# Two constants of a list scheduler: a longer hand-over between engines is counted, and attention's TensorE work is ranked further ahead

## The chip, the cores and the metric

The kernel runs on one core of one Trainium2 chip. The metric is device time in microseconds (us), from one execution to the next, as a median over runs. Engines are called by the profile's names: PE is TensorE (matmuls; PEld its weight loads), DVE is VectorE, ACT is ScalarE, POOL is GpSimd, SP is SyncE, which here only issues the transfers (DMA).

## What is computed

Three stages feed one another: local attention with block summaries (2 batches, 8 heads, 768 positions, head width 64), and two MLPs (1536 tokens, 512 wide, 2048 inside), the first with softplus and the second with a squared ReLU. All is float32.

```
k_sum = k.reshape(B, H, nb, 32, D).max(axis=3)
v_sum = v.reshape(B, H, nb, 32, D).mean(axis=3)
scores_l = scale * q @ k^T, kept where |i - j| < 16
scores_s = scale * q @ k_sum^T + log(32)
a = softmax over [scores_l, scores_s];  attn = a @ [v, v_sum]
x = attn as (1536 tokens, 512)
x = softplus(x @ w_in) @ w_out          (moe)
x = relu(x @ w_in)**2 @ w_out           (moe2)
```

## The kernel before

**The work.** Attention goes over 12 tiles of 128 tokens, t0 to t11 (t0 to t5 are batch 0), each with 24 summary keys and two windows of 96 keys. The queries and keys come in blocks u0 to u5 of 256 tokens. For a block, `tr` transposes on PE (line L361; the first blocks at L397) and copies the result out of PSUM (ACT or DVE, L306 or L308); for keys `kmax` (L369) also takes block maxima on DVE. For a tile, `tile_sc` multiplies queries with keys (L491), and the softmax follows: the mask is added on DVE (L499), the maximum taken on DVE (L530), subtracted on POOL (L532), exponentiated on ACT (L534), summed on DVE (`tot`, L516 to L518) and scaled on POOL (L536). `tile_px` transposes the weights of the softmax in two halves (L547, copied out at L306 or L308), multiplies them with the values (L561), and splits the product into a high part `xh` (L306) and a low part `xl` (L571). `vsum_mm` (L439, copied out at L444) makes the block means of the values once for each batch.

An MLP product takes three matmuls, high times high, high times low, low times high. Each weight block (a step c of 128 inner columns, in and out weight) is therefore split first: ACT or DVE extracts the lowest three bits (L609 on ACT, L611 on DVE), DVE joins bits twice (L614), ACT or POOL scales and copies (L306 or L308), and POOL or DVE subtracts for the low part (L623). `mlp_in` multiplies tokens with the in weight (L664), ACT applies the function (L671) and copies the high part (L678), DVE takes the low part (L680), and `mlp_out` multiplies with the out weight (L701). The first MLP's steps c0 to c3 run on 256 tokens at a time while attention is still going on (stretch A below); all other steps run on 512 tokens.

**What sets the order.** The program collects all operations in a `Plan`, each with the engines that can do it, a duration for each, a due time, and what it reads and writes. `Plan.run` goes through them once, when the program is built. It keeps a clock for each engine, always takes the engine that can start first, and from the operations that are ready on it the one with the earliest due time. Where two engines can do an operation, the one that would end first gets it. A result counts as ready for others at its end plus `SEM`. So the plan's numbers set only an order of instructions for each engine and the choice of engine. On the chip each engine works through its order and waits at each instruction for its inputs. `PEB` is taken off the due time of attention's PE operations alone:

```
op("PE", 0.65, due - PEB, mm, r=[("s", y, hh), "id"], w=[bk], take=bk)
...
ready[u] = max(ready[u], end + self.SEM)
```

`Plan.run` also fills holes: where the plan sees PE idle for over 0.9 us, it puts matmuls that compute nothing there (`warm`, L857). PSUM space for attention's results (the tiles `ab`; the first tiles also use `h`) is handed out in the plan's order; from t2 on there are two such tiles, and a new product has to wait until the old one has been copied out. Transfers are issued from SP in the plan's order; raw weight blocks (`raw`, four places) at L599 and L602, windows of values (`vwin`) at L425, blocks of queries and keys at L350.

## Time and profile before

| | |
|---|---|
| median of 3 runs | 619.96 us (619.87 to 622.35) |
| the profiled execution, its time | 620.8 us |
| its span, first to last instruction | 619.0 us |
| PE busy | 602.5 us (97%) |
| DVE busy | 312.1 us (50%) |
| ACT busy | 288.2 us (47%) |
| POOL busy | 202.0 us (33%) |

1.8 us of the profiled execution lie outside the span. Busy shares are means over the whole span; PE's includes the matmuls that compute nothing.

### The profile page before, as it was taken

How to read it: one execution, taken by the hardware profiler on the slowest of the kernel's cores; microseconds unless marked ns; L12 is line 12 of the kernel's file. 1: busy time of each engine (PE TensorE's matmuls, PEld its weight loads, DVE VectorE, ACT ScalarE, POOL GpSimd, SP SyncE). 2: the span in 40 equal slices, each digit the busy share in tenths (PEclk: the TensorE clock that was granted, in tenths of full speed). 3: DMA queues.
4: the chain of work that ended last, by engine and by line, in shares of the span. 5: the costliest groups of instructions: out<-in, count | busy, mean ns of one | idle time of the engine just before them, and what ended most of it. 6: DMA issues, size and time to landing. Idle time of an engine off the chain costs nothing.

```text
span 619.0 us, 9449 instructions
## 1 busy us (share of the span) xinstructions
PE 602.5 (97%) x3809; PEld 507.5 (82%) x3809; DVE 312.1 (50%) x449; ACT 288.2 (47%) x501; POOL 202.0 (33%) x197
## 2 busy tenths in 40 slices
PE   9798999999999999999999999999999999999996
PEld 7687988999788888888888888888888888888885
DVE  5788999726664133542146652247542533232332
ACT  4686888856653124542247643346412432221220
POOL 5877696535550042331138440116000410000000
PEclk9798999999999999999999999999999999999999
DMA  9999632423541014340024330114100100010011
GB/s 283 243 281 217 162 74 55 116 69 116 166 128 35 0 35 136 103 136 1 0 64 122 120 103 0 35 61 131 47 1 0 69 0 2 0 58 11 20 50 68
DMA packets 64524, 51.34 MB, mean 83 GB/s; under 512 B 36320, under 2 KB 58848, under 8 KB 64480
## 3 DMA queue, kind: packets, MB, share of 16 engines
q1 hardware_dynamic: 64480, 50.73, 28.6%
q8 instruction: 30, 0.49, 0.3%
q14 instruction: 14, 0.11, 0.1%
HBM read 47.58 MB, written 3.15 MB: 82 GB/s over the span
## 4 chain that ended last, share of the span: by engine, by line
PE 84%; DVE 8%; DMA 4%; ACT 2%; SPq 1%; issue 1%; POOL 0%; DVEq 0%; POOLq 0%
PE h L664 40%; PE accp L701 21%; PE acc L701 18%; DMA late<-in_v_dram 2%; DMA vwin<-in_v_dram 2%; DVE raw L614 2%; DVE mx L530 1%; DVE s L499 1%; PE ab L439 1%; PE ab L561 1%; DVE sm L516 1%; SPq L382 1%; PE ab L547 1%; DVE xl L571 0%; DVE sm L517 0%
## 5 line engine op out<-in xcount | busy, mean ns | idle before, releaser
L664 PE MATMUL h<-xh,wih 128*128 128x512 f32 (+1 forms) x432 | 159.9, 370 | 0.0
L664 PE MATMUL h<-xh,wil 128*128 128x512 f32 (+1 forms) x432 | 158.7, 367 | 0.0
L664 PE MATMUL h<-xl,wih 128*128 128x512 f32 (+1 forms) x432 | 158.7, 367 | 0.0
L614 DVE SCALAR_TENSOR_TENSOR raw<-raw 128x512 uint32<-128x512 uint32 x128 | 113.3, 902 | 52.8 <-ACT raw L609 39.8
L664 PEld LDWEIGHTS h<-xh,wih 128*128 128x128 f32 x432 | 81.5, 189 | 14.6 <-issue 0.6
L664 PEld LDWEIGHTS h<-xh,wil 128*128 128x128 f32 x432 | 81.3, 188 | 13.9
L664 PEld LDWEIGHTS h<-xl,wih 128*128 128x128 f32 x432 | 81.4, 188 | 13.7
L673 ACT ACTIVATE e<-h 128x512 f32<-128x512 f32 x48 | 28.8, 599 | 125.4 <-PE h L664 125.4
L675 DVE SCALAR_TENSOR_TENSOR h<-h,e 128x512 f32<-128x512 f32 x48 | 33.5, 698 | 103.2 <-ACT e L673 103.1
L671 ACT ACTIVATE h<-h 128x512 f32<-128x512 f32 (+1 forms) x60 | 29.8, 499 | 83.2 <-PE h L664 83.1
L308 POOL TENSOR_SCALAR wih<-raw 128x512 fp32r<-128x512 f32 x18 | 12.6, 703 | 150.5 <-PE h L664 142.1
L623 POOL TENSOR_TENSOR wol<-raw,woh 128x512 fp32r<-128x512 f32 x30 | 42.6, 1421 | 48.9 <-ACT woh L306 48.3
L623 POOL TENSOR_TENSOR wil<-raw,wih 128x512 fp32r<-128x512 f32 x31 | 42.6, 1374 | 28.9 <-ACT wih L306 27.4
L609 ACT ACTIVATE raw<-raw 128x512 uint32<-128x512 uint16 x59 | 39.3, 670 | 13.2 <-DMA raw<-in_moe_w_out_dram 7.5
L680 DVE TENSOR_TENSOR g1l<-h,g1h 128x512 fp32r<-128x512 f32 (+1 forms) x40 | 24.2, 606 | 31.9 <-ACT g1h L678 31.8
L723 DVE TENSOR_TENSOR part<-accp,part 128x512 f32<-128x512 f32 x24 | 16.0, 686 | 43.5 <-PE accp L701 43.5
L680 DVE TENSOR_TENSOR g2l<-h,g2h 128x512 fp32r<-128x512 f32 x28 | 19.3, 690 | 33.7 <-ACT g2h L678 33.5
L306 ACT ACTIVATE raw<-raw 128x512 f32<-128x512 f32 x41 | 27.5, 673 | 18.7 <-DVE raw L614 18.7
L680 DVE TENSOR_TENSOR g0l<-h,g0h 128x512 fp32r<-128x512 f32 (+1 forms) x40 | 24.1, 605 | 21.1 <-ACT g0h L678 20.9
L678 ACT ACTIVATE g0h<-h 128x512 fp32r<-128x512 f32 (+1 forms) x40 | 21.2, 534 | 16.4 <-DVE h L675 16.0
L536 POOL TENSOR_TENSOR s<-s,sm 128x960 f32<-128x960 f32 (+1 forms) x14 | 22.1, 1580 | 13.9 <-DVE sm L518 13.0
L678 ACT ACTIVATE g1h<-h 128x512 fp32r<-128x512 f32 (+1 forms) x40 | 21.4, 534 | 9.2 <-DVE h L675 8.9
(172 smaller groups left out, 1175.4 us busy)
## 6 DMA issues: line engine op xcount, KB each, us to landing
raw<-in_moe_w_in_dram SPq DMA_DIRECT2D x32, 512.0 KB, 4.2
raw<-in_moe_w_out_dram SPq DMA_DIRECT2D x32, 512.0 KB, 3.4
vwin<-in_v_dram SPq DMA_DIRECT2D x20, 192.0 KB, 5.7
part<-in_k_dram SPq DMA_DIRECT2D x12, 256.0 KB, 4.9
late<-in_v_dram SPq DMA_DIRECT2D x2, 1536.0 KB, 11.3
out_dram<-part SPq DMA_DIRECT2D x12, 256.0 KB, 2.1
part<-in_q_dram SPq DMA_DIRECT2D x10, 256.0 KB, 5.1
vwin<-in_v_dram SPq DMA_DIRECT2D x4, 160.0 KB, 5.2
```

What stands on the lines that cost most here:

```text
L306: nc.scalar.activation(out=out_, in_=in_, func=AF.Copy, **({} if mul is None else {"scale": mul}))
L536: op(("POOL", "DVE"), (1.8 * n + 0.1, 1.75 * n), due, lambda e, sv=sv, rv=rv, spread=spread: tt(e).tensor_tensor(out=sv, in0=sv, in1=sprea ...
L609: nc.scalar.activation(out=lo, in_=q4[:, :, 1], func=AF.Copy, scale=2.0 ** -13, bias=-4095.5 / 8192.0)
L614: nc.vector.scalar_tensor_tensor(out=lo, in0=hi, scalar=n, in1=lo, op0=how, op1=ALU.bitwise_or)
L623: op(("POOL", "DVE"), (1.4, 1.0), dv, lambda e: tt(e).tensor_tensor(out=ws[s][kl], in0=lo.bitcast(F32), in1=ws[s][kh].bitcast(F32), op=ALU ...
L664: nc.tensor.matmul(out=hview(st), lhsT=ws[s][wn][:, w_], rhs=xx[bl][:, kk, o:o + n], start=(kk == 0 and xx is xh and wn == "ih"), stop=(kk ...
L671: op("ACT", ta, due, lambda: nc.scalar.activation(out=hview(st), in_=hview(st), func=AF.Softplus), w=[H_], tab="sp")
L673: op("ACT", ta, due, lambda: nc.scalar.activation(out=e_t[st["g"] % 2], in_=hview(st), func=AF.Relu), r=[H_], w=[("e", st["g"] % 2)])
L675: op("DVE", tv, due, lambda: nc.vector.scalar_tensor_tensor(out=hview(st), in0=hview(st), scalar=0.0, in1=e_t[st["g"] % 2], op0=ALU.max, o ...
L678: op("ACT", ta, due, lambda: nc.scalar.activation(out=gview(st)[0], in_=hview(st), func=AF.Copy), r=[H_] + need, w=gk[0])
L680: op("DVE", tv, due, lambda: nc.vector.tensor_tensor(out=gview(st)[1], in0=hview(st), in1=gview(st)[0].bitcast(F32), op=ALU.subtract), r=[ ...
L701: nc.tensor.matmul(out=o, lhsT=a[:, sl], rhs=b, start=(st["first"] and c == 0 and not (A and m % 2)), stop=(st["last"] and c == 2 and not ...
```

## The change

Both edits are numbers. `SEM` is the time that the plan counts between the end of an operation and the start of one that needs it on any engine. `PEB` is the lead that attention's PE operations get in rank over all other PE operations.

```
-PEB = 40.0
+PEB = 60.0
...
-    SEM = 0.12
+    SEM = 0.3
```

The set of computing operations is the same; their order on each engine, the engine of some of them, and the number of filling matmuls change (53 before, 50 after). Over the whole program these choices differ: the bit extraction runs 59 times on ACT and 5 times on DVE before, 63 times and once after; the low part of a weight 61 times on POOL and 3 times on DVE before, 64 times and never after; one transposed block is copied by DVE before, and three PSUM results of `tile_px` after. The loads of ACT's function tables are 18 in both.

On ACT, where the softmax of t3 (tile `s_133`) meets the second weight block of c2 (`raw_76`, the out weight), this is the order before:

```order
L671 ACTIVATE h_109<-h_109 128x256
L306 ACTIVATE kT<-ab_141 128x4x128
L678 ACTIVATE g0h<-h_109 128x256
L306 ACTIVATE qT_127<-ab_142 128x4x128
L534 ACT_TABLE_LOAD
L534 ACTIVATE s_133<-s_133 128x960
L306 ACTIVATE at_134<-ab_141 120x512
```

And this is the order after, at the same place:

```order
L306 ACTIVATE kT<-ab_141 128x4x128
L671 ACTIVATE h_109<-h_109 128x256
L609 ACTIVATE raw_76<-raw_76 128x512
L306 ACTIVATE qT_127<-ab_142 128x4x128
L678 ACTIVATE g0h<-h_109 128x256
L534 ACT_TABLE_LOAD
L534 ACTIVATE s_133<-s_133 128x960
L306 ACTIVATE at_134<-ab_142 120x512
```

The bit extraction of `raw_76`, which DVE did before, stands on ACT ahead of the copy of a query block, of c1's high part and of t3's exponentials.

On DVE the piece of the difference at the same place shows what left and what stayed (`raw_75` to `raw_77` are the blocks of c2's in, c2's out and c3's in weight):

```order
-L680 TENSOR_TENSOR g0l<-h_109,g0h 128x256
-L614 SCALAR_TENSOR_TENSOR raw_75<-raw_75 128x512
-L611 TENSOR_SCALAR raw_76<-raw_76 128x512
+L680 TENSOR_TENSOR g0l<-h_108,g0h 128x256
+L614 SCALAR_TENSOR_TENSOR raw_75<-raw_75 128x512
+L614 SCALAR_TENSOR_TENSOR raw_76<-raw_76 128x512
+L680 TENSOR_TENSOR g0l<-h_109,g0h 128x256
 L611 TENSOR_SCALAR raw_77<-raw_77 128x512
+L499 TENSOR_TENSOR s_132<-sc,mask 128x480
 L516 TENSOR_REDUCE sm_139<-s_133 128x8
```

The extraction of `raw_77` stays on DVE ahead of t3's sum (L516); that of `raw_76` is gone, and c1's low part (`g0l<-h_109`) now stands behind a join of `raw_76`.

On PE the piece of the difference a little later, where t2's weighted values (L561) and the block means of batch 1 (L439) are made:

```order
 L701 MATMUL accp<-g0h,wol_90 128x256
 L701 MATMUL accp<-g0l,woh_89 128x256
-L361 MATMUL ab_141<-ident,part_69 128x128 x4
+L547 MATMUL ab_142<-ident,s_132 120x128 x4
+L439 MATMUL ab_141<-late,sel 24x128 x24
 L561 MATMUL ab_142<-at_134,vwin_130 64x64 x16
-L439 MATMUL ab_141<-late,sel 24x128 x24
 L664 MATMUL h_108<-xh_71,wih_91 128x256
```

The block means moved ahead of t2's weighted values, and the second half of t2's transposes came down to just ahead of them; the query block's transposes went further up, out of this piece.

## Rows read from the trace of the kernel before

**Rows 1.** The page, part 1: busy us, share of the span, instructions.

```profile
PE 602.5 (97%) x3809; PEld 507.5 (82%) x3809; DVE 312.1 (50%) x449; ACT 288.2 (47%) x501; POOL 202.0 (33%) x197
```

**Rows 2.** Windows: stretch and length, each engine's busy us, then PE's granted clock, DMA.

```profile
22.00:28.50 6.50, 6.50 (x70) 5.26 (x71) 5.09 (x12) 3.00 (x10) 4.81 (x6) 0.56 0.92 199
48.00:56.40 8.40, 6.04 (x95) 4.88 (x94) 7.32 (x10) 3.82 (x9) 4.28 (x5) 0.80 1.01 207
...
60.90:104.00 43.10, 40.56 (x540) 37.52 (x536) 42.76 (x61) 35.81 (x58) 33.38 (x29) 1.00 0.46 109
104.00:146.75 42.75, 42.38 (x464) 41.26 (x465) 24.88 (x41) 30.44 (x54) 18.70 (x15) 1.00 0.30 83
146.75:619.00 472.25, 466.97 (x2066) 384.00 (x2064) 198.82 (x278) 181.76 (x311) 107.18 (x92) 1.00 0.18 58
```

**Rows 3.** The waits of PE over the span: total us, times, longest us.

```profile
PE ab L439 <- DMA late<-in_v_dram: 3.3, 1, 3.3
...
PE accp L701 <- ACT part L713: 0.6, 1, 0.6
```

**Rows 4.** Timeline of PE, 22 to 29 us: start, us, instructions [idle before].

```profile
22.00 2.78 PE L439 MATMUL ab<-late,sel 128*24 128x128 f32 x48 [3.33 <-DMA late<-in_v_dram]
24.70 2.10 PE L857 MATMUL h<-ident 128*128 128x256 bf16 x9
...
28.05 0.60 PE L857 MATMUL h<-ident 128*128 128x256 bf16 x4
```

**Rows 5.** Timeline of ACT, 42 to 53 us.

```profile
42.93 0.38 ACT L678 ACTIVATE g0h<-h 128x256 fp32r<-128x256 f32 x1
43.65 0.60 ACT L306 ACTIVATE qT<-ab 128x512 f32<-128x512 f32 x1 [0.34 <-PE ab L361]
44.27 1.28 ACT L534 ACT_TABLE_LOAD   x1
45.56 1.01 ACT L534 ACTIVATE s<-s 128x960 f32<-128x960 f32 x1
...
52.45 0.69 ACT L609 ACTIVATE raw<-raw 128x512 uint32<-128x512 uint16 x1 [3.57 <-DMA raw<-in_moe_w_out_dram]
```

**Rows 6.** Timeline of DVE, 46 to 51 us.

```profile
46.62 0.43 DVE L611 TENSOR_SCALAR raw<-raw 128x512 uint32<-128x512 uint32 x1 [1.03 <-DMA raw<-in_moe_w_out_dram]
49.01 0.43 DVE L611 TENSOR_SCALAR raw<-raw 128x512 uint32<-128x512 uint32 x1 [1.97 <-DMA raw<-in_moe_w_in_dram]
49.36 1.15 DVE L516 TENSOR_REDUCE sm<-s 128x8 f32<-128x960 f32 x1
```

**Rows 7.** Timeline of PE, 44 to 57 us.

```profile
44.59 1.06 PE L547 MATMUL ab<-ident,s 128*120 128x128 f32 x8 [0.27 <-POOL raw L308]
...
50.06 0.34 PE L561 MATMUL ab<-at,vwin 120*64 120x64 f32 x4 [1.81 <-DMA vwin<-in_v_dram]
50.94 1.18 PE L561 MATMUL ab<-at,vwin 120*64 120x64 f32 x28 [0.54 <-DMA vwin<-in_v_dram]
52.05 2.78 PE L439 MATMUL ab<-late,sel 128*24 128x128 f32 x48
...
56.43 1.03 PE L547 MATMUL ab<-ident,s 128*120 128x128 f32 x8
```

**Rows 8.** Groups by line and shape, 0 to 125 us: count | busy us, mean ns | idle before.

```profile
L611 DVE TENSOR_SCALAR raw<-raw 128x512 uint32<-128x512 uint32 x5 | 4.4, 876 | 3.0 <-DMA raw<-in_moe_w_in_dram 2.0 <-DMA raw<-in_moe_w_out_dram 1.0
L623 DVE TENSOR_TENSOR wol<-raw,woh 128x512 fp32r<-128x512 f32 x2 | 4.1, 2048 | 0.1
L623 DVE TENSOR_TENSOR wil<-raw,wih 128x512 fp32r<-128x512 f32 x1 | 1.1, 1092 | 1.2 <-ACT wih L306 1.2
L308 DVE TENSOR_SCALAR qT<-ab 128x512 f32<-128x512 f32 x1 | 0.7, 678 | 0.0
L444 ACT ACTIVATE vsum<-ab 24x128 f32<-24x128 f32 x8 | 2.2, 270 | 3.9 <-PE ab L439 3.9
L609 ACT ACTIVATE raw<-raw 128x512 uint32<-128x512 uint16 x9 | 6.2, 686 | 6.6 <-DMA raw<-in_moe_w_out_dram 4.2 <-DMA raw<-in_moe_w_in_dram 2.3
```

## The prediction, made before the changed kernel ran

> **What bounds the kernel now.** I read the page first, then PE's waits, then a table of stretches, and last the timelines of the places where an order changed. The page says that PE is busy for 602.5 of 619.0 us, and no other engine for more than about half [rows 1]. So the time is PE's work plus the little that PE waits, and the question is where it waits. The stretches answer that [rows 2]. From 146.75 us to the end PE is busy for 466.97 of 472.25 us, and most of the rest is the tail after the last product; the change cannot make those products shorter. From 104 to 146.75 us PE idles for 42.75 - 42.38 = 0.37 us. From 60.9 to 104 us it idles for 43.10 - 40.56 = 2.54 us, and here DVE is the full engine: 42.76 of 43.10 us. Before that, transfers set the pace: the DMA share is 0.92 and 1.01 in the two stretches shown [rows 2], PE waits 3.3 us for the values of batch 0 [rows 3] and 1.81 and 0.54 us for a window of values [rows 7], and at both places its granted clock falls to the lower level of 1.2 GHz: the means are 0.56 for 22 to 28.5 us and 0.80 for 48 to 56.4 us [rows 2].
>
> So the change can win at most the 2.9 us of waits after 60.9 us, and what it wins or loses around 40 to 57 us, where orders meet transfers that come when they come.
>
> **Up to 36 us: nothing.** The first thirteen load instructions stand in the same order, so the values of batch 0 still land at 22.0 us and PE still starts the block means there [rows 4]. Behind them there are now 16 filling matmuls in one piece instead of nine and four. At the lower clock nine took 2.10 us, 0.23 each, and the four at the full clock 0.60 us [rows 4]. Sixteen take about 3.6 us, some 0.9 us more than the 2.70 us of before; the first transposes of the softmax start later by that. It is absorbed if PE waits again at 45 to 51 us, as it does before [rows 7]. I count 0, with 0.9 us as the bound.
>
> **40 to 57 us: moves in both directions, sum 0.** Two edits of the order meet here.
>
> The first is a loss. ACT now has the bit extraction of `raw_76` ahead of a query block's copy, c1's high part and t3's exponentials. That block lands at about 46.6 us: DVE, which extracted its bits before, sat waiting until then [rows 6]. ACT comes to it at about 43 us, where c1's high part was copied before [rows 5], so it stands for some 3.5 us. After that come the extraction (mean 0.69 us, [rows 8]), the copy (0.60), the high part (0.38), the table load (1.28) and the exponentials (1.01) [rows 5]: 46.6 + 0.7 + 0.6 + 0.4 + 1.3 + 1.0 = 50.6 us, instead of 46.6. But t3's sum on DVE did not start at 46.6 either: DVE itself stood until 49.01 us before `raw_77`, and summed from 49.36 [rows 6]. It still has that wait, and now sums from about 50.6: t3 is late by 1.2 us, not by 4.0. PE feels the stop directly. The first transpose of t2, at 44.59 us before [rows 7], needs the PSUM tile that the held copy releases, at about 47.9 us; c1's out products wait for their low part behind it, and the second transpose for a copy behind the exponentials, at 50.6 + 0.6 = 51.2 us.
>
> The second edit is a gain of the same size. The block means of batch 1 stood behind t2's weighted values, which waited until 50.94 us for their window [rows 7]. They now go ahead, and a landing at 50.9 us no longer holds back their 2.78 us. But by the first edit they start only behind the second transpose, at about 51.7 us, 0.4 us before their old start. What comes next is t3's first transpose, at 56.43 us before [rows 7]. It needs the block means copied out, which ACT does behind the extraction of `raw_78`, whose load landed at 52.4 us [rows 5] and now has a key load of 256 KB queued ahead of it. At the 207 GB/s of this stretch [rows 2] that is 1.2 us: 53.6 + 0.7 (extraction) + 0.7 (a weight copy, taken as long) + 1.1 (four copies of 0.27, [rows 8]) = 56.1 us. PE's own order has the block means (1.4 us at the full clock, half of the 2.78; or 2.78), the weighted values (about 1.2) and c2's product (54.83 to 56.43 before, 1.6 us, [rows 7]) to do first: 51.7 + 4.2 = 55.9 or 57.3 us. So t3's transpose starts at 56.1 to 57.3, against 56.43: I take 56.6, **+0.2 us**, with bounds of -0.3 and +0.9, and 1.3 us more if the query block behind it has to wait for ACT's next table load (1.28 us, [rows 5]) as well.
>
> A clock rule is weighed here. Before, the wait of 1.81 and 0.54 us [rows 7] was followed by a stretch at a mean clock of 0.80 [rows 2]. PE now stands for some 2.5 us up to 47.9 us and for about 1 us before 51.2 us. The Trainium skill (TensorE: Matmul & The Clock Gate, the section on HAM oscillation) says that idle gaps put the array back to half rate and that the loss is half of the time spent so. The trace agrees in kind with its 0.56 and 0.80. By the rows one stretch like that, 0.20 of 8.40 us = 1.7 us of lost clock, is in the time already; whether the new gaps make a second is a rival below.
>
> **60.9 to 146.75 us: lighter DVE, heavier ACT, 0.** In stretch A DVE loses four of five extractions (4.4 us for five) and all three low parts (4.1 + 1.1 us), and gets two more PSUM copies (0.68 us each) [rows 8]: 3.5 + 5.2 - 1.4 = 7.3 us less on the engine that was full. POOL takes the three low parts and ACT the extractions. ACT was busy for 35.81 of 43.10 us [rows 2], so four times 0.69 us fit. That speaks for fewer waits of PE. Against it: PE now gets attention's products as soon as the plan finds them ready, and they stand at the head of its order even where the chip finds them late, with MLP work queued behind. Query block u5 is now transposed ahead of c1's in product on the second 256 tokens, where before it came behind c3's, so its loads are needed sooner. POOL has c5's weight ahead of t5's scaling, on which PE's next transposes hang. The bounds are -2.9 us (all waits gone) and +3 us (as much again). Nothing in the rows puts it on one side: 0.
>
> **After 146.75 us: 0.** PE waited once, 0.6 us, for a PSUM tile to be emptied [rows 3]. The out products of c4 now follow those of c3 directly, so that wait may stay or double: -0.6 to +0.6.
>
> **The sum** against the profiled execution's 620.8 us (span 619.0 and 1.8 around it) is 620.8 + 0 + 0.2 + 0 + 0 = 621.0 us. The median of the runs is 0.84 us below that execution, so the forecast is 620.2 us, no change. What a measurement of this kernel can tell from no change is about 0.5%, 3.1 us: 616.9 and 623.1 are the borders.
>
> **The rivals.**
> - **The stop on ACT is carried on (slower).** If t3's 4.0 us were not swallowed by DVE's own wait, or if ACT's later rows push t4 and t5 as well, then the whole chain of softmaxes shifts by some 3.5 us; in 60.9 to 104 us neither DVE (0.34 us free) [rows 2] nor, with its additions, ACT has room to catch up. It decides once PE's stock of MLP work is used up, and then adds 3.5 us: 623.7 us. For it: the late loads [rows 5, 6]. Against it: DVE's 7.3 us.
> - **The lighter DVE and the earlier block means pay (faster).** PE's waits of 2.9 us after 60.9 us go, and the block means' 1.4 us at full clock are won: 620.2 - 0.2 - 2.9 - 1.4 = 615.7 us. For it: DVE is the full engine exactly where PE waits. Against it: POOL and ACT get what DVE loses, and 2.9 us of 85.9 is little to win back.
> - **A second stretch at the lower clock.** PE's stop before 47.9 us is longer than the 1.81 us that went ahead of the 0.80 stretch [rows 7], and a second stop follows. If they bring one more stretch like that: 620.2 + 1.7 = 621.9 us. For it: both long waits of before have such a stretch behind them [rows 2]. Against it: the new stops stand where one of the two was already. The skill's rule above speaks for it.
> - **The change does nothing that counts.** PE has other work whenever attention is late, so a rank alone moves work and no time: 620 us. This is nearly the forecast and is counted with it.
>
> **How the numbers follow.** Forecast with no effect included 0.44, second slow-clock stretch 0.17, stop carried on 0.21, DVE's relief 0.18. The first two lie inside the borders: same 0.61, slower 0.21, faster 0.18. The forecast's own range is 618.5 to 621.9. The range for 8 in 10 reaches to both outer cases without their far ends: 616.8 to 623.9 us.
>
> **What would show it.** Right: on ACT the extraction (L609) stands before `raw_76` for about 3 us at 43 to 46.6 us; PE has a gap there; L439 of batch 1 comes before L561 of t2 and starts at 51 to 52 us; t3's transposes start at 56 to 57.3 us; DVE is no longer full in 60 to 104 us and PE's waits there remain at 2 to 4 us; the steady part after 150 us is the same length to 1 us. Wrong: PE's waits after 61 us under 1 us or over 6 us; a granted clock under 1.00 anywhere from 57 to 146 us; or transfers landing at other times than before, since every landing above is taken over from the rows.

## The result and the profile after

The changed kernel takes 625.25 us (median of 5 runs, 623.66 to 625.9); before, run beside it, 619.89 us (619.35 to 622.35). The ratio is 1.0073, 95% interval 1.0054 to 1.0092: slower by 0.7%. The forecast was 620.2 us, and 625.25 lies outside its range of 616.8 to 623.9.

The profiled execution of after is its fastest: 623.66 us, a span of 621.5. Against that of before (620.8) it is 2.86 us longer. The rest of the 5.36 us between the medians is the spread of the runs: the median of after is 1.59 us above its profiled execution, that of before 0.91 us below.

The page, part 1, of after (busy us, share of the span, instructions), answers to [rows 1]: PE, though busy for less, has a longer span.

```profile
PE 599.1 (96%) x3806; PEld 505.0 (81%) x3806; DVE 311.2 (50%) x444; ACT 289.1 (47%) x505; POOL 204.1 (33%) x198
```

The windows of after, columns as in [rows 2]:

```profile
22.00:28.50 6.50, 5.26 (x69) 4.25 (x70) 3.80 (x11) 3.30 (x12) 3.49 (x4) 0.74 0.95 181
48.00:56.40 8.40, 7.29 (x120) 6.40 (x120) 7.81 (x12) 7.37 (x14) 5.16 (x5) 1.00 1.16 231
56.40:60.90 4.50, 2.93 (x68) 2.46 (x70) 4.50 (x5) 3.69 (x8) 3.86 (x4) 1.00 0.99 232
60.90:104.00 43.10, 36.40 (x467) 33.84 (x462) 40.12 (x56) 34.46 (x58) 35.20 (x31) 1.00 0.44 109
104.00:146.75 42.75, 42.75 (x517) 41.42 (x516) 22.07 (x39) 31.38 (x54) 15.12 (x9) 1.00 0.25 66
146.75:621.50 474.75, 470.32 (x2096) 387.71 (x2094) 204.05 (x281) 182.17 (x315) 111.12 (x96) 1.00 0.18 59
```

The row that stands out is the one from 60.9 to 104 us: PE idles there for 43.10 - 36.40 = 6.70 us, where it idled for 2.54 [rows 2]. From there to 146.75 us there is no idle time. From 48 to 56.4 us the clock is at its full level, where before's mean was 0.80; from 56.4 to 60.9 us PE idles for 1.57 us, where it idled for 0.02 (the row of before is shown further down).

A finer measure is the starts of c3's in products on PE, one for each 256 tokens. Before: 60.89 us (tokens from 0), 97.33 (from 512), 118.40 (from 768), 145.31 (from 1280), and the last product ends at 614.29. After: 61.15, 102.19, 121.18, 148.94 and 617.07. Up to the first, after loses 0.26 us; from the first to the one on 1280 it takes 87.79 us instead of 84.42, so 3.37 more; behind that 468.13 instead of 468.98, so 0.85 less. The sum is 2.78.

What PE waits for between 60.9 and 146.75 us in after (total us, times, longest):

```profile
PE h L664 <- DVE xl L571: 2.1, 1, 2.1
PE ab L547 <- DVE xl L571: 1.8, 1, 1.8
PE sc L491 <- DVE kaug L416: 1.5, 1, 1.5
PE sc L491 <- DVE s L499: 0.9, 1, 0.9
PE h L664 <- DVE g1l L680: 0.5, 1, 0.5
```

Every releaser is DVE, which is itself no longer full (40.12 of 43.10 us). So its total load doesn't explain that its rows come late; what remains is their place in its queue. The longest wait shows how. Three timelines of after, of DVE, POOL and PE (start, us, operation, in brackets the idle time ahead and its releaser):

```profile
83.16 1.57 DVE L614 SCALAR_TENSOR_TENSOR raw<-raw 128x512 uint32<-128x512 uint32 x1
...
87.30 0.68 DVE L308 TENSOR_SCALAR xh<-ab 128x512 fp32r<-128x512 f32 x1
87.90 3.58 DVE L614 SCALAR_TENSOR_TENSOR raw<-raw 128x512 uint32<-128x512 uint32 x1
91.40 0.68 DVE L571 TENSOR_TENSOR xl<-ab,xh 128x512 fp32r<-128x512 f32 x1
```
```profile
82.39 1.79 POOL L532 TENSOR_TENSOR s<-s,mx 128x960 f32<-128x960 f32 x1 [0.25 <-DVE mx L530]
84.15 0.95 POOL L459 TENSOR_SCALAR kaug<-kT 128x384 f32<-128x384 f32 x1
...
87.73 1.78 POOL L532 TENSOR_TENSOR s<-s,mx 128x960 f32<-128x960 f32 x1
89.49 1.45 POOL L459 TENSOR_SCALAR kaug<-kT 128x384 f32<-128x384 f32 x3
```
```profile
92.14 0.39 PE L664 MATMUL h<-xl,wih 128*128 128x256 f32 x1 [2.07 <-DVE xl L571]
```

PE needs t5's low part `xl`. Its inputs are there at 87.98 us, but a join of c5's out weight stands in front, for a product that runs after 146 us. The next join, which starts at 92.00 us with POOL idle, takes 0.68 us; this one takes 3.58, until 0.54 us after the last of POOL's four rows (one L532, three L459) has ended at 90.94.

### The profile page after: what moved, and what is told of

It reads as the page before. It is cut to its first block, busy times and chain, and to the rows that moved or that the text cites. A ratio compares the mean times of both kernels' runs of the same rounds, so it can differ in the third digit from the quotient of the medians.

```text
span 621.5 us, 9452 instructions
## 1 busy us (share of the span) xinstructions
PE 599.1 (96%) x3806; PEld 505.0 (81%) x3806; DVE 311.2 (50%) x444; ACT 289.1 (47%) x505; POOL 204.1 (33%) x198
## 4 chain that ended last, share of the span: by engine, by line
PE 86%; DMA 4%; DVE 4%; ACT 2%; issue 1%; SPq 1%; POOL 1%; DVEq 0%; POOLq 0%
PE h L664 41%; PE accp L701 23%; PE acc L701 18%; DMA late<-in_v_dram 2%; DMA raw<-in_moe_w_in_dram 2%; DVE raw L614 1%; PE ab L547 1%; PE ab L561 1%; SPq L382 1%; PE sc L491 1%; DVE s L499 0%; PE ab L439 0%; DVE mx L530 0%; SPq L602 0%; PE h L857 0%
## 5 line engine op out<-in xcount | busy, mean ns | idle before, releaser
L664 PE MATMUL h<-xl,wih 128*128 128x512 f32 (+1 forms) x432 | 158.8, 368 | 2.1 <-DVE xl L571 2.1
L664 PE MATMUL h<-xh,wih 128*128 128x512 f32 (+1 forms) x432 | 159.7, 370 | 0.5 <-DVE g1l L680 0.5
L664 PE MATMUL h<-xh,wil 128*128 128x512 f32 (+1 forms) x432 | 158.7, 367 | 0.0
L614 DVE SCALAR_TENSOR_TENSOR raw<-raw 128x512 uint32<-128x512 uint32 x128 | 119.1, 949 | 38.2 <-ACT raw L306 18.8
L664 PEld LDWEIGHTS h<-xl,wih 128*128 128x128 f32 x432 | 81.3, 188 | 16.0 <-DVE xl L571 2.3
L664 PEld LDWEIGHTS h<-xh,wih 128*128 128x128 f32 x432 | 81.4, 188 | 15.0 <-DVE g1l L680 0.7
L664 PEld LDWEIGHTS h<-xh,wil 128*128 128x128 f32 x432 | 81.3, 188 | 13.9
L308 POOL TENSOR_SCALAR wih<-raw 128x512 fp32r<-128x512 f32 x16 | 10.9, 683 | 133.2 <-PE h L664 130.1
L623 POOL TENSOR_TENSOR wil<-raw,wih 128x512 fp32r<-128x512 f32 x32 | 44.0, 1378 | 29.7 <-ACT wih L306 28.6
L623 POOL TENSOR_TENSOR wol<-raw,woh 128x512 fp32r<-128x512 f32 x32 | 45.1, 1415 | 23.2 <-ACT woh L306 22.6
L609 ACT ACTIVATE raw<-raw 128x512 uint32<-128x512 uint16 x63 | 42.1, 678 | 13.7 <-DMA raw<-in_moe_w_out_dram 7.1
L306 ACT ACTIVATE raw<-raw 128x512 f32<-128x512 f32 x44 | 29.5, 673 | 8.9 <-DVE raw L614 8.8
L308 POOL TENSOR_SCALAR raw<-raw 128x512 f32<-128x512 f32 x20 | 14.5, 727 | 36.8 <-DVE raw L614 36.8
```

What stands on the lines that cost most here:

```text
L306: nc.scalar.activation(out=out_, in_=in_, func=AF.Copy, **({} if mul is None else {"scale": mul}))
L308: tt(e).tensor_scalar(out=out_, in0=in_, scalar1=1.0 if mul is None else mul, scalar2=1.0, op0=ALU.mult, op1=ALU.mult)
L609: nc.scalar.activation(out=lo, in_=q4[:, :, 1], func=AF.Copy, scale=2.0 ** -13, bias=-4095.5 / 8192.0)
L614: nc.vector.scalar_tensor_tensor(out=lo, in0=hi, scalar=n, in1=lo, op0=how, op1=ALU.bitwise_or)
L623: op(("POOL", "DVE"), (1.4, 1.0), dv, lambda e: tt(e).tensor_tensor(out=ws[s][kl], in0=lo.bitcast(F32), in1=ws[s][kh].bitcast(F32), op=ALU ...
L664: nc.tensor.matmul(out=hview(st), lhsT=ws[s][wn][:, w_], rhs=xx[bl][:, kk, o:o + n], start=(kk == 0 and xx is xh and wn == "ih"), stop=(kk ...
```

## The experiments

For most runs the program makes both lists of operations, with the constants of before and of after, and then emits a third one mixed from them (`mix`); with `return after` it is the kernel after, row for row. A list entry is (operation, engine, PSUM place, filling matmuls). `behind(op, log, ((a, b), ...))` moves operation a, with what depends on it, behind b; `ahead` moves a, with what it depends on, ahead of b. The code below is cut to the lines that differ. Operations have numbers: 177 is c3's in product on tokens from 0, 580 that on 1280. The joins are 139, 141 (c4 in), 146, 148 (c4 out), 153, 155 (c5 in), 160, 162 (c5 out), 547, 549 (c9 in), 589, 591 (c6 in), low parts 150, 157, 164.

| run | median us | ratio to before, interval |
|---|---|---|
| after's order to 61 us, then before's | 620.65 | 0.9993 [0.9983, 1.0004] |
| before's order to 61 us, then after's | 624.38 | 1.0052 [1.0036, 1.0068] |
| before's order, after's engines | 620.66 | 0.9997 [0.9987, 1.0007] |
| after's order, before's engines | 623.63 | 1.0044 [1.0027, 1.0061] |
| SEM alone | 624.22 | 1.0059 [1.0040, 1.0079] |
| two joins ahead, in before | 622.12 | 1.0031 [1.0020, 1.0043] |
| weight work ahead, in before | 630.07 | 1.0152 [1.0136, 1.0168] |
| POOL's weight work behind | 626.63 | 1.0096 [1.0077, 1.0115] |
| c5's out weight behind | 625.38 | 1.0072 [1.0059, 1.0086] |
| weight work behind, placing 1 | 632.56 | 1.0194 [1.0178, 1.0209] |
| placing 1 with c6 | 625.41 | 1.0084 [1.0063, 1.0105] |
| placing 2 (all through) | 627.30 | 1.0116 [1.0101, 1.0131] |
| placing 3 | 622.27 | 1.0027 [1.0015, 1.0040] |
| placing 4 | 626.09 | 1.0081 [1.0066, 1.0096] |
| placing 5 | 622.47 | 1.0029 [1.0014, 1.0045] |
| placing 6 | 619.54 | 0.9983 [0.9972, 0.9995] |
| before's order to 147 us, then after's | 620.02 | 0.9989 [0.9980, 0.9999] |

**Where: the cut at 61 us.**

```diff
-    return after
+    first, rest = after, before
+    n = [x[0] for x in first].index(177)
+    head = first[:n]
+    seen = {x[0] for x in head}
+    return head + [x for x in rest if x[0] not in seen]
```

> All engines follow the order of after up to the place where c3's in product on the first 256 tokens stands on PE (61.15 us in after), and from there the remaining instructions in the order of before. Theory 'order in 61 to 104 us' (weight work of c4 and c5 ahead of t5 to t9's softmax on DVE and POOL): the loss is gone, 619.5 to 621 us. Rival 'ACT's stop at 43 to 46.6 us is carried on': the loss stays, since it came before the cut: 623.5 to 625.5 us. Rival 'the granted clock' (a second stretch at half rate before 61 us that the profiled run of after happened not to have): half of it, 621.5 to 622 us.

The reverse run has `first, rest = before, after`.

> The reverse: the order of before up to c3's in product on the first 256 tokens, from there that of after. 'Order in 61 to 104 us': 623 to 625 us, with PE idle for 5.5 to 7 us in 60.9 to 104 us. 'ACT's stop': 619.5 to 620.5 us. 'The granted clock': about 623 us, without the half-rate part of the loss.

The first is 620.65 us, the second 624.38: ahead of the cut nothing is lost, and behind it most or all (1.0052 beside 1.0073 for after, whose intervals overlap). The first has ACT's stop of 43 to 46.6 us and loses nothing by it, so that rival falls. The second has PE's waits of after (its window, then two of PE's waits; L711, L618 and L594 are L664, L571 and L547):

```profile
60.90:104.00 43.10, 36.84 (x458) 33.84 (x451) 39.33 (x55) 32.16 (x55) 34.14 (x29) 0.96 0.43 107
```
```profile
PE h L711 <- DVE xl L618: 2.1, 1, 2.1
PE ab L594 <- DVE xl L618: 1.8, 1, 1.8
```

Its granted clock is 0.96 here, as in the profiles of SEM alone, of placing 3 and of the runs with POOL's or c5's weight work behind; that is 0.04 x 43.10 = 1.7 us of clock, where after's own profile shows 1.00. In this run the fall comes right behind the wait of 2.07 us: from 92.6 to 96 us the matmuls start 0.21 us apart, before and after that 0.12, and from c3's first product to the one on 1280 it takes 89.27 us, 1.48 more than in after. In after's profile the same two waits bring no fall. So such waits are followed by a stretch at 1.2 GHz in some executions only, and this may be the 1.59 us by which the median of after exceeds its profiled run, whose mean clock is 0.996 (its other four executions have 0.991 to 0.994). In which stretch those four lost their clock isn't on record; it can also be ahead of 61 us.

**Engine or order.**

```diff
+SWAP = (136, 142, 145, 150, 156, 159, 161, 284, 295, 430, 458)
...
-    return after
+    order, engines = before, after
+    eng = {i: e for i, e, b, f in engines}
+    return [(i, eng[i] if i in SWAP else e, b, f) for i, e, b, f in order]
```

> The order of before in the whole program; only the eleven instructions whose engine differs between 54 and 105 us run where after has them (two extractions L611 from DVE to ACT, two low parts L623 from DVE to POOL, three copies of attention from ACT to DVE and one from DVE to ACT, three scalings or high parts between ACT and POOL). Naive working (DVE's lost work is time won): 617 to 619 us. Theory 'lock' (DVE's joins L614 are held while POOL works, so moving low parts to POOL stretches them): 621 to 624 us, with L614's mean rising from 1.09 us to 1.3 us or more. Theory 'order': 619 to 621 us, since the engines are not the cause.

The reverse has `order, engines = after, before`.

> The order of after in the whole program; the same eleven instructions run where before has them. 'Order': the loss stays or grows, 624 to 628 us, since DVE gets its work back and the weight work still stands ahead of t5 to t9. 'Lock': 620 to 622 us, L614's mean back at 1.1 us. 'ACT's stop': 624 to 626 us (the extraction that stops ACT is not among the eleven).

The engines alone do nothing (0.9997), and the order alone does most of it (1.0044). Whether the engines add to it in after's order (1.0044 beside 1.0073) isn't settled: the two intervals overlap a little. The groups of the joins from 60.9 to 104 us, in after and then in the first of these runs (L662 is its L614):

```profile
L614 DVE SCALAR_TENSOR_TENSOR raw<-raw 128x512 uint32<-128x512 uint32 x12 | 16.2, 1355 | 0.6 <-POOL raw L308 0.6
```
```profile
L662 DVE SCALAR_TENSOR_TENSOR raw<-raw 128x512 uint32<-128x512 uint32 x9 | 11.9, 1322 | 0.3 <-ACT raw L657 0.3
```

In before these were nine joins with 9.8 us, and DVE also had two extractions (1.8) and two low parts (4.1) in the stretch. With these 5.9 us gone and the order kept, the nine joins take 2.1 us more, now that POOL has the low parts. So a third of the relief is given back by joins that POOL holds up (below), and PE gains nothing by the rest.

**The lock by itself.** Five groups behind the last instruction of before:

```diff
+        for beside, work in ((None, join), (sub, join), (sub, low), (sub, bits), (fill, join)):
+            nc.vector.memset(f(0)[0:1, 0:1], 0.0)
+            nc.gpsimd.tensor_copy(out=f(3)[0:1, 0:1], in_=f(0)[0:1, 0:1])
+            if beside:
+                for _ in range(3):
+                    beside()
+            nc.vector.tensor_copy(out=f(0)[0:1, 1:2], in_=f(3)[0:1, 0:1])
+            for _ in range(3):
+                work(0)
```

> Before, with five small groups behind its last instruction, DVE and POOL alone at work: three joins (L614's form) with POOL idle; three joins, three low parts that read PSUM, and three bit extractions (one SBUF input) each beside three subtractions on POOL (128x512, both inputs in SBUF); three joins beside three fills on POOL that read nothing. Theory 'lock': joins alone 0.65 to 0.8 us each; beside the subtractions the first takes until POOL's last one has ended, about 3.5 to 4 us, the others 0.65 to 0.8; the reads from PSUM are untouched, about 0.7 us; the extractions are held as the joins are. Rival 'bandwidth' (both slow one another down): each of the three joins 1 to 1.5 us and POOL's subtractions longer than their 1.3 us alone. Beside the fills: held as well if any work on POOL holds the joins, 0.65 to 0.8 us if only work that reads does.

DVE's timeline, then POOL's (each row three instructions, where x3):

```profile
616.34 2.15 DVE L867 SCALAR_TENSOR_TENSOR raw<-raw 128x512 uint32<-128x512 uint32 x3
619.12 4.90 DVE L867 SCALAR_TENSOR_TENSOR raw<-raw 128x512 uint32<-128x512 uint32 x3
624.57 2.14 DVE L870 TENSOR_TENSOR raw<-h,raw 128x512 f32<-128x512 f32 x3
628.49 4.21 DVE L874 TENSOR_SCALAR raw<-raw 128x512 uint32<-128x512 uint32 x3
633.26 2.15 DVE L867 SCALAR_TENSOR_TENSOR raw<-raw 128x512 uint32<-128x512 uint32 x3
```
```profile
618.87 4.60 POOL L877 TENSOR_TENSOR woh<-wih,wil 128x512 fp32r<-128x512 f32 x3
624.33 3.94 POOL L877 TENSOR_TENSOR woh<-wih,wil 128x512 fp32r<-128x512 f32 x3
628.35 4.07 POOL L877 TENSOR_TENSOR woh<-wih,wil 128x512 fp32r<-128x512 f32 x3
632.99 1.68 POOL L880 MEMSET raw<- 128x512 f32 x3
```

Alone a join takes 0.69 us, a subtraction on POOL 1.25. Beside the subtractions the three take 1.56, 1.63 and 1.64 us, the first from 619.12 to 620.67 while POOL's first ends at 620.12, and POOL's second and third take 1.59 instead of 1.25. By these durations the rival 'bandwidth' (1 to 1.5 us a join, POOL longer) came nearer than the lock as I expected it, with the first join behind all three. What speaks for a lock is who waits: POOL's first, with the join beside it from 619.12 us, takes its 1.25 us as if alone, and the join ends 0.55 us behind it. So one stands while the other runs, and here they took it in turn. Reads from PSUM (0.69) and joins beside fills (0.69) are untouched, extractions are held (1.37 to 1.41, where one takes 0.43 in [rows 6]). The Trainium skill (SBUF — State Buffer, Who interferes with whom) says that a VectorE instruction with two SBUF inputs contends with a GpSimd instruction that reads SBUF, and not with one that only writes; the runs agree (1.56 to 1.64 us a join beside POOL's subtractions, 0.69 beside its fills). How many of POOL's instructions a join has to wait for isn't settled. In after POOL's rows follow one another without a gap (each starts 0.03 us ahead of the last one's end), and the join of 87.90 us waited for four of them. But the join of 83.16 us ended at 84.73, 0.55 us behind one L532, though the next row followed just as closely; that one, an L459, took 0.95 us instead of 0.50. So the missing gap doesn't decide it (here there were 0.08 us).

**Which constant.**

```diff
-PEB = 60.0
+PEB = 40.0
```

> SEM = 0.3 with PEB = 40. (PEB = 60 with SEM = 0.12 gives the order of before in every row, so it needs no run.) If the longer hand-over is what sends weight work ahead: 623 to 626 us. If it takes both constants (the higher rank on PE at the longer hand-over): 619.5 to 621.5 us.

1.0059 beside 1.0073 for both constants, and the intervals overlap: the longer hand-over does most or all of it. At the old hand-over PEB = 60 changes no row on any engine; at the new one it does move rows, and what that costs is within the noise.

**Joins put ahead in before.** Base: the order of before with the engines of after (0.9997).

```diff
+    return ahead(op, log, ((160, 376), (162, 296)))
```

> The counterpart in small: the order of before with the engines of after (620.66 us as measured), with only c5's out weight's two joins put ahead on DVE, the first to just ahead of t7's mask addition, the second to just ahead of t5's low part, as after has it (its scaling on ACT goes with them). 'The order on DVE': the joins delay what stands behind by what they are held, 1 to 4 us; PE has stock for part of it, so 621 to 623 us. 'PE's own order': no change, 620 to 621 us.

Two rows, with the scaling on ACT that goes with them, cost 1.0031 - 0.9997, about 2.1 us. The joins are held, the first for 2.03 us at 79.25, and t5's low part comes behind the second, as DVE's timeline shows (L695 is L614, L652 is L571). The profile is of the longest of nine executions, 626.38 us, so its times are not compared.

```profile
89.30 1.66 DVE L695 SCALAR_TENSOR_TENSOR raw<-raw 128x512 uint32<-128x512 uint32 x1
90.88 0.68 DVE L652 TENSOR_TENSOR xl<-ab,xh 128x512 fp32r<-128x512 f32 x1
```

The larger version of the same:

```diff
+    return ahead(op, log, ((146, 281), (153, 281), (155, 361), (148, 362), (160, 376), (162, 296), (547, 365),
+                           (157, 282), (150, 379), (164, 366)))
```

> The counterpart: the order of before with the engines of after (620.66 us as measured), PE's order untouched, and only the joins and low parts of c4's out weight, c5's two weights and c9's first join go ahead, about to where after has them (c5's out weight ahead of t5's low part). 'Weight work ahead of attention': 622 to 625 us, with PE waiting for xl and for t6's softmax between 75 and 100 us. 'PE's own order': no change, 620 to 621 us.

It overdid it: 630.07 us, far over the expected 622 to 625. DVE also stood for 5.2 us before joins whose inputs had not come from POOL and ACT; in after that is 0.6 us. It shows the sign only.

**Weight work put behind in after.** PE's order is that of after in all that follows.

```diff
-    return after
+    return behind(op, after, ((156, 282), (157, 382), (150, 379), (164, 382)))
```

> After with four instructions moved on POOL alone (c5's in weight, scaling and low part, behind t5's and t6's last scaling; the low parts of c4's and c5's out weights behind t7's subtraction and t6's last scaling); DVE, ACT and PE untouched. If POOL's order is what makes attention late: 622 to 623.5 us. If DVE's joins are: 624.5 to 625.5 us, no change from after.

626.63: no better than after. Its profile has a new wait of 3.1 us, behind a load for which ACT stood 5.2 us, so the time by itself proves little; but after's three longest waits are still there (1.9, 1.8 and 1.5 us), so the place of these rows on POOL alone doesn't make them.

```diff
+    return behind(op, after, ((162, 381), (160, 296), (164, 382), (588, 440), (589, 449), (590, 440), (591, 450)))
```

> After, with only c5's out weight (its two joins, behind t5's low part and t7's sum) and in its wake c6's in weight put behind; everything else, PE's order too, as in after. If the two joins that stand right ahead of t5's low part (1.57 and 3.58 us) are the larger part of the loss: 622 to 623.5 us and PE's wait of 2.1 us for t5's xl gone. If the loss is spread over all the weight work: 623.5 to 625 us. 'PE's own order': 625 us.

625.38: no gain. PE's wait of 2.1 us for `xl` is gone, and one of 2.1 us for an MLP low part has come. One weight alone only moves the wait.

```diff
+    return behind(op, after, ((162, 450), (160, 448), (155, 296), (148, 437), (146, 362), (153, 376),
+                              (549, 507), (547, 449), (157, 382), (150, 439), (164, 451)))
```

> The order and engines of after, PE's order untouched; only weight work that MLP products after 146 us need (the joins and low parts of c4's out weight and c5's two weights, the joins of c9's in weight) goes behind attention's rows on DVE and POOL, about where before has it (c5's out weight behind t9's maximum, for example). Theory 'weight work ahead of attention on DVE and POOL': from c3's first in product to its last (t0 to t1280) 84 to 85.5 us instead of 87.8, and 620 to 622 us. Rival 'PE's own order' (attention's products stand at the head of PE's queue and hold MLP work up): it is unchanged here, so 624 to 625.5 us.

632.56, against 620 to 622 expected. To c3's product on tokens from 512 it took 36.56 us (before 36.44, after 41.04), as the theory says; then a new wait undid it. Its rows on ACT and PE:

```profile
112.97 0.65 ACT L688 ACTIVATE raw<-raw 128x512 uint32<-128x512 uint16 x1 [5.28 <-DMA raw<-in_moe_w_in_dram]
```
```profile
116.42 1.11 PE L626 MATMUL ab<-ident,s 128*120 128x128 f32 x4 [9.83 <-DVE xl L650]
```

c6's extraction was left in its place on ACT, while its load waited for c5's block to leave the shared raw place. The next two runs put c6 back too (`(588, 510), (589, 461), (590, 407), (591, 519), (161, 440)` added), and then go on behind 104 us.

> As the run with the weight work behind attention, but with c6's in weight (two instructions on ACT, two joins on DVE) also put back to about where before has it: in that run it stood ahead of t7's and t8's rows while its load still waited for c5's block to leave the shared raw place. 'Weight work ahead of attention on DVE and POOL': the 36.6 us from c3's first in product (t0) to the one on t512 stay (41.0 in after), the wait of 9.8 us behind it is gone, 84 to 86 us from t0 to t1280, and 620 to 622 us. Rival 'PE's own order': 624 us or more.

625.41. The 36.7 us stay, the wait of 9.83 is gone, and two others of 2.07 and 2.22 us come, again made by moved rows: ahead of the second DVE stands 2.67 us before a join of c6, at 116.92 us, for ACT.

```diff
-(162, 450), (549, 507), (164, 451), (589, 461), (591, 519)
+(162, 398), (549, 402), (164, 454), (589, 408), (591, 520)
```

> After, PE's order untouched, with the weight work of c4's out weight, c5, c9 and c6 behind attention's and the MLP products' rows on DVE also between 104 and 118 us, where the run before it had two waits of PE made by the moved rows themselves (2.07 us for t7's low part behind c5's second join, 2.22 us for c0's low part behind a join of c6 that waited for ACT). 'The order on DVE': both waits go, 84 to 85.5 us from c3's first in product to its last (88.35 in that run, 87.79 in after), 620 to 622 us. Rival 'PE's own order of after cannot be fed in time, wherever the weight work stands': 623.5 us or more.

627.3. Those two waits went, as expected, and ACT stood 4.08 us before c6's late load, PE 4.63 us behind it.

```diff
-(162, 398), (164, 454), (588, 510), (589, 408), (590, 407), (591, 520)
+(162, 461), (164, 512), (588, 522), (589, 523), (590, 528), (591, 531)
```

> After, PE's order untouched, as the run before, with what made its wait of 4.63 us taken away: there c6's extraction stood on ACT for 4.08 us before its load, because c5's low part had left the raw place late. Now c6's rows on ACT and DVE go behind t11's exponentials and sum, c5's second join behind t8's low part, its low part on POOL behind t10's scaling. 'The order on DVE, ACT and POOL': no wait of PE over 1.5 us between 85 and 145 us, 83.5 to 85.5 us from c3's first in product to its last (87.79 in after, 84.42 in before), 620 to 622 us. 'PE's own order of after cannot be fed in time': 623.5 us or more.

622.27, ratio 1.0027: of after's 0.73% some 0.46 are gone. The longest waits left were 1.47 us for the block maxima and 1.15 us behind ACT, and placing 4 takes these on.

```diff
+(139, 370), (141, 230), (163, 418), (465, 418), (463, 418), (412, 418)
```

> As the third placing (622.27 us, 1.0027), PE's order of after still untouched, with its two longest waits of PE taken on: c4's first join goes behind the copies of the block maxima for t6 and t7 and its second behind c0's low part (PE waited 1.47 us at 67 us for those copies), and on ACT c5's high part, which stood 2.44 us before a join that POOL held for 2.0 us, goes behind c3's results, which go ahead of t9's copies (PE waited 1.15 us at 118.4 us). 'The order on DVE, ACT and POOL is all of it': 620.3 to 621.3 us, within 0.15% of before. 'Part of it is PE's own order': no gain over the third placing, 621.8 to 622.8 us.

626.09: the two waits shrank (0.61 us and none), but ACT stood before c3's second result, which PE had finished at 115.7 us, until a later product on PE had ended (4.52 us, until 121.52). Why it waits for that one isn't settled.

```diff
-(465, 418), (463, 418), (412, 418)
```

> The fourth placing without the reordering of c3's results on ACT: there the two waits taken on shrank (1.47 to 0.61 us, 1.15 to 0) and c3's product on t768 came 55.7 us after the one on t0 (57.5 in before, 60.0 in after), but ACT then stood 4.52 us before c3's second result and PE 3.82 us behind it. 'The order on DVE, ACT and POOL is all of it': no wait of PE over 1 us between 62 and 145 us, 83 to 84.5 us from c3's first in product to its last, 620 to 621.3 us. 'Part of it is PE's own order': 621.8 us or more.

622.47, ratio 1.0029. From c3's first product to the one on 768 it takes 55.98 us (before 57.51, after 60.03); from there to the one on 1280 30.73 (26.91 and 27.76), with one wait of 1.81 us. Its origin is again a moved row: c6's join on DVE is held by POOL, ACT stands before c6's scaling, and the functions of the MLP products behind it on ACT come late. The join takes 2.03 us from 126.47 on, ACT stands 1.62 us for it, until 128.53, and PE's row is

```profile
131.97 0.38 PE L745 MATMUL h<-xh,wih 128*128 128x256 f32 x1 [1.81 <-DVE g0l L761]
```

```diff
-(588, 522), (589, 523), (590, 528), (591, 531)
+(588, 530), (589, 478), (590, 483), (591, 538)
```

> The fifth placing (622.47 us) with c6's four rows further behind: there c6's join was held by POOL for 2.03 us, ACT stood 1.62 us for it ahead of c0's and c1's functions, and PE waited 1.81 us for the low part behind them. Now its extraction stands behind t10's high part on ACT, its joins behind c1's and t11's low parts on DVE. 'The order on DVE, ACT and POOL is all of it': the wait of 1.81 us goes, 82.5 to 84.5 us from c3's first product to its last (84.42 in before), 620 to 621.2 us. 'Part of it is PE's own order': 621.8 us or more although no wait of over 1 us is left between 62 and 145 us.

619.54 us, ratio 0.9983 [0.9972, 0.9995]: below what both theories gave, and below before. The wait is gone; from c3's first product to the last it takes 83.51 us (before 84.42, after 87.79), and the rest 468.13 as in after. The window, the group of the joins in it and all of PE's waits from 60.9 to 146.75 us that the view lists:

```profile
60.90:104.00 43.10, 41.12 (x548) 38.59 (x546) 37.29 (x57) 35.90 (x59) 32.66 (x31) 1.00 0.41 95
```
```profile
L695 DVE SCALAR_TENSOR_TENSOR raw<-raw 128x512 uint32<-128x512 uint32 x8 | 10.7, 1340 | 0.0
```
```profile
PE ab L628 <- DVE xl L652: 0.7, 1, 0.7
PE sc L572 <- DVE kaug L497: 0.6, 1, 0.6
PE ab L442 <- DMA part<-in_q_dram: 0.6, 1, 0.6
PE h L745 <- DVE g0l L761: 0.4, 1, 0.4
```

So with PE's order of after, moving weight work on DVE, ACT and POOL alone takes back the whole loss: PE's order by itself needn't cost anything. It is the last of seven placings, most of them made from the waits of the one before; whether before's order of PE would gain as much from such a search was not tried. A join is held as long as in after (1340 and 1355 ns), but eight stand in this stretch instead of twelve. What counts is less how long a join is held than who stands behind it.

**A mix of both.** The cut at 580 instead of 177, with `first, rest = before, after`.

> The order of before up to c3's in product on the last 256 tokens (145.3 us), then that of after. From that product to the end the profile took 468.98 us in before and 468.13 us in after, so 619.0 to 619.8 us, 0.5 to 0.9 us below before run beside it. If that difference comes from what was prepared earlier: no gain, 620 to 622 us.

620.02 against 620.58 beside it, 0.9989 [0.9980, 0.9999]: 0.1% faster than before, in the size that the two profiles show for the steady part (0.85 us). Placing 6 has this and the better order ahead of it, and is the fastest version measured; both gains are far less than the 0.5% that was set as the border.

## Why the prediction was wrong

**Up to 36 us: 0, with a premise that failed.** The values of batch 0 were to land at 22.0 us as before; the block means start at 23.24 us, since the transfer landed later (a wait of 5.1 us against 3.3). Over all twenty profiles they start between 21.98 and 24.22 us, so this moves from one execution to the next. The sixteen filling matmuls took 2.23 us instead of 3.6 (by the prediction's own 0.23 each it would have been 3.7), with the clock's mean from 22 to 28.5 us at 0.74 against 0.56. The first transposes of the softmax started at 28.02 us, 1.42 later than before, over the bound of 0.9; by 61 us no more than 0.26 us was left of it.

**40 to 57 us: the stop right, the sum right by luck.** ACT's timeline of after, answering to [rows 5], and PE's, answering to [rows 7]:

```profile
46.63 0.67 ACT L609 ACTIVATE raw<-raw 128x512 uint32<-128x512 uint16 x1 [2.29 <-DMA raw<-in_moe_w_out_dram]
...
49.35 1.01 ACT L534 ACTIVATE s<-s 128x960 f32<-128x960 f32 x1
```
```profile
47.91 0.62 PE L547 MATMUL ab<-ident,s 128*120 128x128 f32 x4 [0.99 <-ACT qT L306]
...
50.90 0.65 PE L547 MATMUL ab<-ident,s 128*120 128x128 f32 x4 [0.90 <-ACT at L306]
51.48 1.51 PE L439 MATMUL ab<-late,sel 128*24 128x128 f32 x48
...
55.54 0.60 PE L547 MATMUL ab<-ident,s 128*120 128x128 f32 x4
...
58.72 0.65 PE L547 MATMUL ab<-ident,s 128*120 128x128 f32 x4 [1.32 <-DVE xl L571]
```

ACT stood 2.29 us until 46.63 (predicted: 3.5 us, until 46.6), t2's transposes came at 47.91 and 50.90 (47.9 and 51.2), the block means at 51.48 (51.7). All this is near. But t3's first transpose came at 55.54, not at 56.1 to 57.3: 0.89 us earlier than before instead of 0.2 later, below the bound of -0.3. The load for which ACT stood ahead of the block means' copies landed at 52.77 us, not at 53.6, and the block means ran at the full clock. What was won was lost again by 61 us, as this row of before shows beside that of after above:

```profile
56.40:60.90 4.50, 4.48 (x86) 3.74 (x84) 4.14 (x6) 4.21 (x8) 4.28 (x4) 1.00 1.09 244
```

PE, busy for 4.48 us there, was busy for 2.93, and its longest wait, 1.32 us, was for a low part on DVE behind a join of 1.78 us. So the 0.26 us that c3's first product shows come near the +0.2 by luck. One pair of profiles can't tell so little either: in the others this product starts anywhere from 59.54 to 63.44 us. What the run with after's order up to 61 us does tell is that this part costs nothing clear of noise: 0.9993, that is -0.4 us, between -1.1 and +0.2. Of the stretches shown only that from 22 to 28.5 us has a part at the lower clock in after (0.26 x 6.50 = 1.7 us of clock).

**60.9 to 146.75 us, "lighter DVE, heavier ACT, 0": this is the step that failed.** It measured +3.37 us in the profiled pair, over the bound of +3, and up to some 1.6 us more in the typical run, if that is where the rest was lost. PE's 6.70 us of idle time are also over the 6 us that the prediction had named as a sign of being wrong. Three things in the step were wrong. First, the 7.3 us by which DVE was to get lighter were counted over 0 to 125 us [rows 8] and at the durations of before. Over that window it did get lighter by 105.62 - 99.80 = 5.82 us of busy time; but from 60.9 to 104 us, where it was full and PE waits, by no more than 42.76 - 40.12 = 2.64, though 5.9 us of extractions and low parts had left: twelve joins stand there instead of nine, at 1.36 us each instead of 1.09. Second, a relief of DVE was taken to be a relief of PE: with the engines swapped and the order kept it was worth nothing (0.9997). Third, the working saw "POOL has c5's weight ahead of t5's scaling", and on DVE looked only at what left. What counted was what had come ahead: joins of c4's, c5's, c9's and c6's weights, needed only after 146 us, in front of t5's to t9's rows and the MLP low parts on which PE hangs. The plan does this by its rule: of what is ready it takes the earliest due, and with a longer hand-over attention's chain of softmax steps is ready later, so that weight work is all that is ready. That is read from the code; no run here shows it by itself. That the order behind 61 us is the cause is shown by the cut; that it is the weight work's place, by two joins put ahead in before (2.1 us lost) and by placing 6 (all of it back, PE's order untouched). The prediction also charged the rank with it ("PE now gets attention's products as soon as the plan finds them ready"); PEB by itself changes no row, and placing 6 loses nothing with PE's order of after.

**After 146.75 us: 0 ± 0.6, measured -0.85.** A little out, on the good side.

**The rivals.** The stop carried on: no, the run with the stop and before's order behind it takes 620.65 us. That its price, 623.7 us, is the time of after's profiled execution is chance. The lighter DVE pays: no. A second stretch at the lower clock: perhaps part of the loss in the runs other than the profiled one, but where the 0.96 rows show it, it lies in 60.9 to 104 us, behind PE's waits there, and not at 48. That DVE would no longer be full was listed as a sign that the forecast holds; with PE's waits all ending in DVE rows it was a sign of the opposite.

## What to carry to other kernels

When a list scheduler's numbers change, look on each engine for work that isn't urgent and now stands ahead of a row for which the bounding engine waits; a lighter engine is no gain if its queue is in a worse order. A VectorE instruction with two SBUF inputs beside a busy GpSimd can be held until GpSimd's instruction ends, and at times for several of them: here 1.57 us for one and 3.58 for four, instead of 0.68. What that costs depends on who stands behind it. And work moved out of the way has its own chain (a shared buffer, a load, another engine's queue): of seven placings of it four ended no faster than the kernel after, and only the last beat the kernel before, by 0.2%.

## What had not been expected of the hardware

A held join doesn't always wait for all that POOL has to do. Beside three subtractions with 0.08 us between them they took turns: 1.56 to 1.64 us for a join of 0.69, and POOL's instructions too were lengthened, 1.25 to 1.59 us. In after one join waited for four POOL rows without a gap (3.58 us) and another, at 83.16 us, for one only, though the next followed as closely; what decides between the two no run here shows.

The same wait of 2.07 us on PE was followed in one profile (before's order to 61 us, then after's) by a stretch of matmuls that start 0.21 us apart instead of 0.12, and in another (after) by none.
